# Scores of one head over all 128 rows, plain products for twelve units, globals' outputs in DRAM, and a new order

## The chip, the cores and the metric

The kernel runs on one core of a Trainium2 chip. TensorE multiplies matrices, VectorE and ScalarE do elementwise work, GpSimd helps with some of it, and SyncE (SP) issues most of the DMAs. The metric is the device time of one execution in microseconds (us); the time quoted is the median of several.

## What is computed

Attention for 8 batches of 8 heads, with 512 local and 32 global positions of 64 elements each, followed by a two-layer network over all 4352 tokens. Local queries see the local keys within 32 positions and all global keys; global queries see every key.

```python
k_all = np.concatenate([k_g, k_l], axis=2)
v_all = np.concatenate([v_g, v_l], axis=2)
s_g = scale * np.matmul(q_g, k_all.transpose(0, 1, 3, 2))
out_g = np.matmul(sm(s_g), v_all)
s_ll = scale * np.matmul(q_l, k_l.transpose(0, 1, 3, 2))
s_ll = np.where(np.abs(pos[:, None] - pos[None, :]) <= 32, s_ll, -1e9)
s_l = np.concatenate([scale * np.matmul(q_l, k_g.transpose(0, 1, 3, 2)), s_ll], axis=-1)
out_l = np.matmul(sm(s_l), v_all)
attn_out = np.concatenate([out_g, out_l], axis=2)        # sm is the softmax
x = attn_out.transpose(0, 2, 1, 3).reshape(B * S, H * D) # 4352 x 512
out = gelu(x @ w_in) @ w_out                             # 512 -> 2048 -> 512
```

## The kernel before

**Units and pieces.** A unit is a batch, a half of its 512 local positions and a pair of heads: 64 units, four to a block of 256 tokens. A piece of the network is one such block, 16 of them, and a last one ("g") of the 256 global tokens. In the network, `ml_hc` makes hidden tiles of 256 columns and `ml_o` the outputs of 512 columns; each product is done three times, since an operand is split into a high part in a fast format (`F32R`) and a low part that holds the rest: high by high, high by low, low by high.

**Attention of a unit.** `st_tk` and `st_tq` transpose keys and queries (for the first eight units, `st_tkn` and `st_tqn` do it on TensorE). `st_k1` and `st_q1` copy the high parts, `st_k2` and `st_q2` subtract to get the low parts; the four lie in one tile `kq`, held once. A head's 64 elements fill half of the 128 rows, so the two heads of a pair lie one above the other. `st_s` makes the scores: two windows of 192 and 224 keys, three products, two heads, so twelve products over 64 rows each, alternating between the upper and lower rows. `st_m` masks and takes the extreme, `st_e` exponentiates, `st_n`, `st_nf`, `st_ns` normalise, `st_t` transposes the weights in seven steps, `st_ah` and `st_al` split them, `st_vc` and `st_vl` split the values, `st_o` multiplies in two groups of four products, and `st_c` and `st_x` add the parts. `st_sg` makes the scores of the global queries over the same keys with two products, from `gs`, which holds high and low parts of the queries of both heads with zeros between.

**Plain units.** Units 0 to `NF32` - 1 (the first 8) keep 32-bit operands instead: one plain product in place of three, by `st_q0`, `st_k0`, `st_s` with its `prods` of one pair, `st_sg0`, `st_a0`, `st_o0` and `st_c0`. There is no split on VectorE or ScalarE and no adding up.

**Globals.** `gu_min` to `gu_yl` finish the global queries of a batch, two heads at a time. `gu_yl` adds its last two parts straight into `xg`, a tile that lives until piece "g" reads it (`ml_xh`).

**Weights.** They come as 64-bit numbers (512 KB per DMA, 32 of them by `w_load`), are rebuilt by `w_1` and `w_2` on ScalarE and `w_3` on VectorE, and split by `w_4` and `w_5`. All are used from the first piece on, so they are all prepared in the first tenth of the run.

**The order.** Nothing is ordered by hand. `step` gives each step its engines, durations (`DUR`), due time (with offsets in `OFF`, `OFF0`, `UO`, `WO`, `XO`), needs, the buffers that it takes and frees, and for DMAs a number of issues and a `size`. A planner then simulates all engines and the DMA, picks the ready step due first on each, and fixes one order per engine. An engine executes that order strictly: a step that waits holds up what is behind it. `AHEAD`, `FA`, `PW` and `PU` place attention against the network.

Of the kernel before, what the change touches and what calls it, by code (L numbers as in the profile page):

```python
# [19 lines left out]
NB = 10  # L20
# [39 lines left out]
}  # L60
OFF0 = {
# [7 lines left out]
PW = 7.45  # L69
PA = 14.0  # L70
UO = [-392.3, -324.5, -466.6, -352.7, -219.4, -4.3, 79.2, -212.3, 297.9, -231.0, -224.0, -213.8, -190.2, -142.1, -206.7, -54.7]
WO = [-233.6, -272.1, 18.8, 79.4, -468.3, -440.1, 10.1, -401.7, 160.7, 127.2, 284.8, 552.5, 98.0, 88.9, -36.8, -133.1, -19.5, 157.0, 203.3, 10.3, 3.9, -137.0, -448.4, 17.1, -86.0, 50.4, 66.1, -73.3, 84.2, -14.7, -33.4, 3.9]
FA = 122.95
PU = 9.25
NF32 = 8
# [22 lines left out]
    ('gagl', (0, 0)): -47.6, ('gagl', (0, 1)): 17.8, ('gah', (0, 0), 0): 36.0, ('gah', (0, 0), 1): 34.5,  # L98
    ('gah', (0, 1), 0): -22.0, ('gah', (0, 1), 1): 38.1, ('gal', (0, 0), 0): -245.5, ('gal', (0, 0), 1): 91.2,
    ('gal', (0, 1), 0): 137.9, ('gal', (0, 1), 1): 13.8, ('gex', (0, 0)): 53.2, ('gex', (0, 1)): -193.4,  # L100
# [7 lines left out]
    ('glv', (0, 1), 0): 62.5, ('glv', (0, 1), 1): -201.2, ('glv', (1, 0), 0): -62.3, ('glv', (1, 0), 1): -12.2,  # L108
    ('gmin', (0, 0)): 276.7, ('gmin', (0, 1)): -18.9, ('gn', (0, 0)): -31.4, ('gn', (0, 1)): 12.5,
    ('go', (0, 0), 0): 1.7, ('go', (0, 0), 1): 229.8, ('go', (0, 1), 0): -314.7, ('go', (0, 1), 1): -76.3,  # L110
    ('gsh', (0, 0), 0): -60.2, ('gsh', (0, 0), 1): -125.5, ('gsh', (0, 1), 0): -74.6, ('gsh', (0, 1), 1): 15.3,
    ('gsl', (0, 0), 0): 39.4, ('gsl', (0, 0), 1): 83.0, ('gsl', (0, 1), 0): 28.1, ('gsl', (0, 1), 1): -71.6,
    ('gt', (0, 0)): 79.7, ('gt', (0, 1)): -124.9, ('gvc', (0, 0), 0): -116.3, ('gvc', (0, 0), 1): -243.4,
    ('gvc', (0, 1), 0): -55.5, ('gvc', (0, 1), 1): 56.6, ('gvc', (1, 0), 0): 66.2, ('gvl', (0, 0), 0): -40.7,
    ('gvl', (0, 0), 1): -73.6, ('gvl', (0, 1), 0): -2.3, ('gvl', (0, 1), 1): -173.1, ('gvl', (1, 0), 0): 139.3,
    ('gx', (0, 0), 0): -103.3, ('gx', (0, 0), 1): 81.1, ('gx', (0, 1), 0): -105.6, ('gx', (0, 1), 1): 50.1,
    ('gyh', (0, 0), 0): -41.4, ('gyh', (0, 0), 1): 27.2, ('gyh', (0, 1), 0): 248.2, ('gyh', (0, 1), 1): -30.0,
    ('gyl', (0, 0), 0): -233.3, ('gyl', (0, 0), 1): 138.1, ('gyl', (0, 1), 0): 36.2, ('gyl', (0, 1), 1): 43.6,
# [1283 lines left out]
```

## Time and profile before

| | us |
|---|---|
| median of 3 runs | 1043.84 |
| lowest and highest | 1042.81, 1045.48 |
| the profiled execution, its own time | 1045.36 |
| its span, first to last instruction | 1043.6 |

The profiled execution has a mean granted clock of 0.985. Times inside it are counted from the span's start. In a row of a group the first number after the bar is the busy time of all its instructions in us, then the mean of one in ns; then follows the idle time of the engine ahead of them and what ended it. In a time line the columns are start, length (from the first start to the last end, of as many as stand behind "x"), engine, line and operation. Matmuls overlap, so what one costs is read from one start to the next and not from its length.

### The profile page before, as it was taken

To read this page: it belongs to the slowest core of one execution; us is meant where nothing else is said; L and a number is where in the kernel's file an instruction comes from. 1 tells how busy PE (TensorE), PEld (TensorE's weight loads), DVE (VectorE), ACT (ScalarE), POOL (GpSimd) and SP (SyncE) were. 2 spreads that over 40 slices of the span, in tenths; PEclk is the share of its full clock that TensorE was granted. 3 is DMA by queue.
4 is the path that set the end of the run, shared out by engine and by line. 5 is a ranking of instruction groups with operands and counts; after the bars stand their busy time and mean duration, and the time that the engine had idled before them with its cause. 6 is when DMAs were issued, how large, how long until landed. Compare 5 with 4: busy or idle time off the path is not lost.

```text
span 1043.6 us, 21145 instructions
## 1 busy us (share of the span) xinstructions
PE 1014.7 (97%) x7100; PEld 903.6 (87%) x7100; DVE 668.0 (64%) x2046; ACT 749.2 (72%) x1613; POOL 349.6 (33%) x397
## 2 busy tenths in 40 slices
PE   7679999999999999999999999999999999999998
PEld 3468899998899999899899989999899989999897
DVE  5777868874787658775787658785787658641100
ACT  5788878877888678776788678776788678853221
POOL 3022433234233433234232433334232433233121
PEclk9689999999999999999999999999999999999999
DMA  7777232223222222222222232222322232101000
GB/s 192 207 219 253 37 84 49 61 46 82 45 43 60 56 68 44 57 45 60 65 45 61 54 69 42 60 42 60 67 44 58 56 69 50 32 12 32 1 21 21
DMA packets 264796, 69.64 MB, mean 67 GB/s; under 512 B 250096, under 2 KB 258288, under 8 KB 264688
## 3 DMA queue, kind: packets, MB, share of 16 engines
q1 hardware_dynamic: 263536, 67.91, 28.4%
q8 instruction: 56, 0.92, 0.4%
q10 hardware_dynamic: 1152, 0.39, 0.1%
q14 instruction: 52, 0.43, 0.1%
HBM read 59.31 MB, written 8.91 MB: 65 GB/s over the span
## 4 chain that ended last, share of the span: by engine, by line
PE 90%; SPq 3%; DMA 3%; DVE 2%; ACT 1%; issue 1%; DVEq 0%; ACTq 0%
PE h L922 12%; PE acc L954 12%; PE acc L956 12%; PE h L924 12%; PE acc L955 12%; PE h L923 12%; PE o L722 5%; PE s L615 5%; PE t L686 3%; DMA wpair<-in_moe_w_out_dram 2%; PE go L855 2%; PE sg L766 1%; PE t L687 1%; DMA raws<-in_q_l_dram 1%; SPq L459 1%
## 5 line engine op out<-in xcount | busy, mean ns | idle before, releaser
L310 POOL TENSOR_TENSOR gl<-gf,gh 128x512 fp32r<-128x512 f32 x135 | 178.0, 1318 | 410.3 <-ACT gh L300 267.7
L922 PE MATMUL h<-xx,w 128*128 128x256 f32 x1088 | 313.1, 288 | 0.0
L924 PE MATMUL h<-xx,w 128*128 128x256 f32 x1088 | 304.3, 280 | 0.9 <-DVE w L310 0.9
L923 PE MATMUL h<-xx,w 128*128 128x256 f32 x1088 | 303.9, 279 | 0.0
L954 PE MATMUL acc<-w,gh 128*128 128x512 f32 x544 | 219.2, 403 | 0.0
L956 PE MATMUL acc<-w,gh 128*128 128x512 f32 x544 | 214.6, 394 | 0.0
L955 PE MATMUL acc<-w,gl 128*128 128x512 f32 x544 | 214.5, 394 | 0.0
L922 PEld LDWEIGHTS h<-xx,w 128*128 128x128 f32 x1088 | 204.9, 188 | 9.5 <-issue 0.4
L923 PEld LDWEIGHTS h<-xx,w 128*128 128x128 f32 x1088 | 204.9, 188 | 6.6
L924 PEld LDWEIGHTS h<-xx,w 128*128 128x128 f32 x1088 | 204.7, 188 | 1.3 <-DVE w L310 1.3
L479 ACT ACT_TABLE_LOAD x127 | 162.9, 1283 | 2.3
L300 ACT ACTIVATE gh<-gf 128x512 fp32r<-128x512 f32 x108 | 68.2, 632 | 97.2 <-PE acc L956 96.8
L310 POOL TENSOR_TENSOR vs<-vr,vs 128x512 fp32r<-128x512 f32 x56 | 74.5, 1329 | 154.9 <-DVE vs L302 47.5
L956 PEld LDWEIGHTS acc<-w,gh 128*128 128x128 f32 x544 | 102.0, 188 | 24.8
L479 ACT ACTIVATE gf<-h 128x512 f32<-128x512 f32 x136 | 81.2, 597 | 50.6 <-PE h L924 28.4
L954 PEld LDWEIGHTS acc<-w,gh 128*128 128x128 f32 x544 | 102.1, 188 | 14.3 <-issue 0.3
L955 PEld LDWEIGHTS acc<-w,gl 128*128 128x128 f32 x544 | 102.4, 188 | 12.6
L479 ACT ACTIVATE a_t<-a_t,sm 128x192 f32<-128x192 f32 x240 | 110.1, 460 | 2.8 <-DVE sm L634 1.2
L634 DVE CUSTOM_DVE_ANT_0 a_t<-s,mask 128x192 f32<-128x192 f32 x240 | 77.1, 368 | 42.7 <-PE s L615 42.6
L706 DVE TENSOR_TENSOR at<-t,at 128x512 fp32r<-128x512 f32 (+1 forms) x112 | 66.5, 613 | 44.7 <-ACT at L300 44.3
L300 ACT ACTIVATE at<-t 128x512 fp32r<-128x512 f32 (+1 forms) x112 | 58.9, 539 | 22.8 <-PE t L689 16.2
L722 PE MATMUL o<-at,vs 128*128 128x256 f32 x448 | 73.3, 286 | 0.0
(139 smaller groups left out, 1555.4 us busy)
## 6 DMA issues: line engine op xcount, KB each, us to landing
wpair<-in_moe_w_in_dram SPq DMA_DIRECT2D x16, 512.0 KB, 6.2
wpair<-in_moe_w_out_dram SPq DMA_DIRECT2D x16, 512.0 KB, 6.4
raws<-in_v_l_dram SPq DMA_DIRECT2D x64, 128.0 KB, 2.4
out_dram<-ob SPq DMA_DIRECT2D x32, 256.0 KB, 2.3
raws<-in_k_l_dram SPq DMA_DIRECT2D x224, 36.0 KB, 2.0
vr<-in_v_l_dram SPq DMA_DIRECT2D x112, 64.0 KB, 2.2
raws<-in_q_l_dram SPq DMA_DIRECT2D x224, 32.0 KB, 1.9
vr<-in_v_l_dram SPq DMA_DIRECT2D x56, 32.0 KB, 2.2
```

Of the source, the lines that this page charges most:

```text
L300: nc.scalar.activation(out=out, in_=in_, func=AF.Copy)
L310: (nc.vector if e == "v" else nc.gpsimd).tensor_sub(**kw)
L479: nc.scalar.activation(func=func, **kw)
L634: nc.vector.tensor_tensor_reduce(out=a_t[:, j, aoff[half][i]:aoff[half][i] + w], in0=s[:, c:c + w], in1=masks[half][:, c:c + w], scale=-SC ...
L706: nc.vector.tensor_sub(out=at[:, 1], in0=st.pop((u, "t", j))[:, :n * P].rearrange("p (n q) -> p n q", q=P), in1=at.bitcast(F32)[:, 0])
L722: nc.tensor.matmul(out=o[:, :, qsl], lhsT=l.rearrange("p s e -> p (s e)"), rhs=r, start=(n == 0), stop=(n == 3), skip_group_check=True)
L922: nc.tensor.matmul(out=h, lhsT=hi, rhs=xh, start=(c == 0), stop=False, skip_group_check=True)
L923: nc.tensor.matmul(out=h, lhsT=hi, rhs=xl, start=False, stop=False, skip_group_check=True)
L924: nc.tensor.matmul(out=h, lhsT=lo, rhs=xh, start=False, stop=(c == NCC - 1), skip_group_check=True)
L954: nc.tensor.matmul(out=acc[t], lhsT=gh[:, f % 2, tsl], rhs=hi, start=(f == a), stop=False)
L955: nc.tensor.matmul(out=acc[t], lhsT=gl[:, f % 2, tsl], rhs=hi, start=False, stop=False)
L956: nc.tensor.matmul(out=acc[t], lhsT=gh[:, f % 2, tsl], rhs=lo, start=False, stop=(f == b - 1))
```

## The change

Six things are changed.

1. **Scores.** `kq` grows from 2 x 320 + 2 x 256 to 2 x 320 + 4 x 256 columns. For head j, the rows of that head hold the high part of the keys and the other 64 rows the low part. Queries: `q1` has the high part in both halves of the rows (the second copy by the new `st_q3`), `q2` has the low part in the head's own rows and zeros in the others (written once). `q1` times keys then gives high by high and high by low in one product over 128 rows, `q2` times keys the third. So `st_s` does eight products over 128 rows. Each of `st_k1`, `st_k2`, `st_q1`, `st_q2` and `st_q3` becomes two instructions on 64 partitions.
2. **Globals' queries.** `gs` has seven slots of 32 columns with zeros between; the queries of all heads lie on all 128 rows, so `load_g` moves twice the bytes and `st_tg` transposes 256 in place of 128 columns. `st_sg` still does two products.
3. **Plain units.** `NF32` is 12: units 8 to 11 (first half of batch 1) are plain too. They take keys and queries straight from the transposed tiles and values straight from `vr`; `st_tc1` prepares the plain global queries of batch 1.
4. **Globals' outputs.** `gu_yl` adds in place, `gu_w` writes each result of 128 x 32 to DRAM, and one read (`gu_r`) brings all of them into the memory of `vr` before piece "g". `xg` goes.
5. **Planner's prices.** New durations for the changed steps, and larger sizes for the loads of keys, queries and values.
6. **Order.** All offsets are new, as are `AHEAD` (21.61 to 23.43), `FA` (122.95 to 108.93), `PW` (7.45 to 8.01) and `PU` (9.25 to 8.86).

```diff
-    "tk": 0.65, ..., "tg": 0.32, "k1": {"a": 0.47, "v": 0.31}, "k2": 0.5, "q1": {"v": 0.3, "a": 0.41}, "q2": 0.42,
-    "tgh": 0.62, "tgl": 0.77, "s": 0.97, ...
+    "tk": 0.65, ..., "tg": 0.5, "k1": {"a": 0.9, "v": 0.62}, "k2": 1.0, "q1": {"v": 0.6, "a": 0.82}, "q3": {"v": 0.6, "a": 0.82}, "q2": 0.84, ...
+    "tgh": 0.62, "tgl": 0.77, "s": 0.87, ...
-NF32 = 8
+NF32 = 12
...
-            kq = late["kq"] = xp.tile([P, 2 * NB * 32 + 2 * CH], F32R, name="kq", tag="kq")
+            kq = late["kq"] = xp.tile([P, 2 * NB * 32 + 4 * CH], F32R, name="kq", tag="kq")
+            late["k"] = kq[:, 0:2 * NB * 32].rearrange("p (j w) -> p j w", j=2)
...
-    gs = cp.tile([P, NP, P], F32R, name="gs")
+    gs = cp.tile([P, NP, 7, 32], F32R, name="gs")
...
-        late["xg"] = lp.tile([P, NP, CH], F32, name="xg")
...
     def st_q1(e, u):
-        copy(e, keys_queries("q1"), st[u, "qt"])
+        q = keys_queries("q1")
+        for j in range(2):
+            own_, other = head(j)
+            copy(e, q[own_, j], st[u, "qt"][own_])
+
+    def st_q3(e, u):
+        q = keys_queries("q1")
+        for j in range(2):
+            own_, other = head(j)
+            copy(e, q[other, j], st[u, "qt"][own_])
...
     def st_k2(e, u):
-        sub(e, out=late["k2"], in0=st.pop((u, "kt")).rearrange("p c e -> p (c e)"), in1=late["k1"].bitcast(F32))
+        k, t = late["k"], st[u, "xkt"].rearrange("p c e -> p (c e)")
+        for j in range(2):
+            own_, other = head(j)
+            sub(e, out=k[other, j], in0=t[own_], in1=k[own_, j].bitcast(F32))
...
+    def st_tc1(e, b):
+        late["gs1"] = g = xp.tile([P, NP, 2, SG], F32, name="gs1", tag="kq")
+        nc.vector.memset(g, 0.0)
+        for j in range(2):
+            pr = slice(64 * j, 64 * j + 64)
+            copy(e, g[pr, :, j], st["qgt", b][pr, j::2])
...
-            for n, (qq, kk) in enumerate(prods):
+            for n in range(1 if plain else 2):
                 for jj in range(2):
-                    pr = slice(64 * jj, 64 * jj + 64)
-                    nc.tensor.matmul(out=st[u, "s", jj][:, c:c + w], lhsT=qq[pr, qt * P:qt * P + P], rhs=kk[pr, k0:k0 + w],
...
+                    if plain:
+                        pr = slice(64 * jj, 64 * jj + 64)
+                        l, r = st[u, "qt"][pr, qt * P:qt * P + P], st[u, "kt"][pr, k0:k0 + w]
+                    else:
+                        l, r = late["q2" if n else "q1"][:, jj, qt * P:qt * P + P], late["k"][:, jj, k0:k0 + w]
+                    nc.tensor.matmul(out=st[u, "s", jj][:, c:c + w], lhsT=l, rhs=r,
...
-            nc.vector.tensor_add(out=late["xg"][pr, p, b * SG:b * SG + SG], in0=st[g, i, "x"][pr, j, 0, :], in1=st[g, i, "c"][pr])
+            nc.vector.tensor_add(out=st[g, i, "c"][pr], in0=st[g, i, "x"][pr, j, 0, :], in1=st[g, i, "c"][pr])
+
+    def gu_w(e, g, i):
...
+        nc.sync.dma_start(out=late["xgd"][:, p, b * SG:b * SG + SG], in_=st[g, i, "c"])
+
+    def gu_r(e):
+        late["xg"] = vr.rearrange("p s i j e -> p (s i j e)").rearrange("p (n w) -> p n w", n=NP)
+        nc.sync.dma_start(out=late["xg"], in_=late["xgd"])
...
-                step(("lk", u), load_kn, (u, m), LKE[n], s0 - 15.0, [], [], issues=2 + half + 1 + m // 2, size=0.2 * m, ...)
+                step(("lk", u), load_kn, (u, m), LKE[n], s0 - 15.0, [], [], issues=2 + half + 1 + m // 2, size=0.25 * m, ...)
-            step(("lv", u), load_v, (u, NP), LVE[half], f0 - 18.0, [], [], issues=9, size=1.4, ...)
+            step(("lv", u), load_v, (u, NP), LVE[half], f0 - 18.0, [], [], issues=9, size=1.8, ...)
...
+            step(("q3", u), st_q3, (u,), "va", s0 - 2.2, [("tq", u), ("q1", u)], [("q3", u)], qb, port=n >= NPE)
+                step(("gw", g, i), gu_w, (g, i), "s", g0 + 8.0 + 2 * i, [("gyl", g, i)], [], [("gc", (g, i))], issues=1, size=0.02)
```

More of the change, by code (lines that the diff above doesn't have):

```diff
@@ L110 @@
[L110 to L114, printed above, removed]
@@ L365, in keys_queries @@
         if "kq" not in late:
-            kq = late["kq"] = xp.tile([P, 2 * NB * 32 + 2 * CH], F32R, name="kq", tag="kq")
-            late["k1"], late["k2"] = kq[:, 0:NB * 32], kq[:, NB * 32:2 * NB * 32]
-            late["q1"], late["q2"] = (kq[:, 2 * NB * 32 + i * CH:2 * NB * 32 + (i + 1) * CH] for i in range(2))
+            kq = late["kq"] = xp.tile([P, 2 * NB * 32 + 4 * CH], F32R, name="kq", tag="kq")
+            late["k"] = kq[:, 0:2 * NB * 32].rearrange("p (j w) -> p j w", j=2)
+            late["q1"], late["q2"] = (kq[:, 2 * NB * 32 + 2 * i * CH:2 * NB * 32 + 2 * (i + 1) * CH].rearrange("p (j w) -> p j w", j=2) for i in range(2))
+            for j in range(2):
+                pr = slice(64 - 64 * j, 128 - 64 * j)
+                nc.vector.tensor_copy(out=late["q2"][pr, j].rearrange("p (x w) -> p x w", w=32), in_=a_ts[0][pr, 0, 224:256].unsqueeze(1).to_broadcast([64, CH // 32, 32]))
         return late[name]
@@ L484, in st_tk @@
         t = ap_.tile([P, NB, 32], F32, name="kt", tag="kt")
-        st[u, "kt"] = t
+        st[u, "kt" if place.get(u, NF32) < NF32 else "xkt"] = t
+        if (u, "kt") in st:
+            st[u, "kt"] = t.rearrange("p c e -> p (c e)")
         g = 4 + half
@@ L592, in st_tgl @@
         for j in range(2):
-            pr, hi, lo = gsv(j)
-            nc.vector.tensor_sub(out=lo, in0=qgt[pr], in1=hi.bitcast(F32))
+            nc.vector.tensor_sub(out=gs[:, :, 4 * j + 2], in0=qgt[:, j::2], in1=gs.bitcast(F32)[:, :, 4 * j])
+    def st_tc1(e, b):
+        late["gs1"] = g = xp.tile([P, NP, 2, SG], F32, name="gs1", tag="kq")
+        nc.vector.memset(g, 0.0)
+        for j in range(2):
+            pr = slice(64 * j, 64 * j + 64)
+            copy(e, g[pr, :, j], st["qgt", b][pr, j::2])
+        late["gs1"] = g.rearrange("p n j w -> p n (j w)")
     def windows(half):
@@ L609, in st_s @@
         c = 0
-        prods = [(st[u, "qt"], st[u, "kt"])] if (u, "kt") in st else [(late[x], late[y]) for x, y in (("q1", "k1"), ("q2", "k1"), ("q1", "k2"))]
+        plain = (u, "kt") in st
         for i, (k0, w, qt) in enumerate(windows(half)):
-            for n, (qq, kk) in enumerate(prods):
+            for n in range(1 if plain else 2):
                 for jj in range(2):
-                    pr = slice(64 * jj, 64 * jj + 64)
-                    nc.tensor.matmul(out=st[u, "s", jj][:, c:c + w], lhsT=qq[pr, qt * P:qt * P + P], rhs=kk[pr, k0:k0 + w],
-                                     start=(i == 0 and n == 0), stop=(i == 1 and n == len(prods) - 1), skip_group_check=True)
+                    if plain:
[4 more added lines that the diff above has]
+                    nc.tensor.matmul(out=st[u, "s", jj][:, c:c + w], lhsT=l, rhs=r,
+                                     start=(i == 0 and n == 0), stop=(i == 1 and (plain or n == 1)), skip_group_check=True)
             c += w
@@ L755, in st_sg @@
         st[u, "sg"] = s
-        for n, kk in enumerate([st[u, "kt"]] if (u, "kt") in st else [late["k1"], late["k2"]]):
+        for n, kk in enumerate([st[u, "kt"]] if (u, "kt") in st else [late["k"][:, j] for j in range(2)]):
             if half == 0:
@@ L763, in st_sg @@
                 r = 64 * (p % 2)
-                nc.tensor.matmul(out=o[r:r + 64], lhsT=gs0[:, p, :], rhs=rhs, start=True, stop=True)
+                nc.tensor.matmul(out=o[r:r + 64], lhsT=(late["gs1"] if b else gs0)[:, p, :], rhs=rhs, start=True, stop=True)
             else:
-                nc.tensor.matmul(out=o, lhsT=gs[:, p, :], rhs=rhs, start=(n == 0), stop=(n == 1))
+                nc.tensor.matmul(out=o, lhsT=gs[:, p, 3 * n:3 * n + 4].rearrange("p x w -> p (x w)"), rhs=rhs, start=(n == 0), stop=(n == 1))
     def gcols(u):
@@ L1055, in pv @@
             return [(x[0], pu, *x[1:]) for x in names] if pu else []
-        if half == 0 and p == 0 and n < NF32:
+        if half == 0 and p == 0 and n < NPE:
             step(("lg", b), load_g0, (b,), "s", s0 - 12.0, takes=[("gvr", "q")], issues=1, size=0.08, after=("lk", u))
@@ L1066, in attn_mlp @@
             step(("tgl", b), st_tgl, (b,), "v", s0 - 5.0, [("tgh", b)], [], [("qt", ("g", b))])
+            if n < NF32:
+                step(("tc1", b), st_tc1, (b,), "v", s0 - 5.2, [("tg", b), ("tq", units[3])], [], [("qt", ("g", b))], dur="tgl")
         pair = units[n - 1] if odd else u
@@ L1072, in attn_mlp @@
                 z = units[n - 1 - units[n - 1][2] % (2 if units[n - 1][1] in QUAD else 4)] if n else None
-                step(("lk", u), load_kn, (u, m), LKE[n], s0 - 15.0, [], [], issues=2 + half + 1 + m // 2, size=0.2 * m, after=("lk", z) if n else None)
-                step(("lq", u), load_qn, (u, m), LQE[n], s0 - 14.0, [], [], issues=2, size=0.18 * m, after=("lq", z) if n else None)
+                step(("lk", u), load_kn, (u, m), LKE[n], s0 - 15.0, [], [], issues=2 + half + 1 + m // 2, size=0.25 * m, after=("lk", z) if n else None)
+                step(("lq", u), load_qn, (u, m), LQE[n], s0 - 14.0, [], [], issues=2, size=0.22 * m, after=("lq", z) if n else None)
             step(("tk", u), st_tkn, (u,), "t", s0 - 5.0, [("lk", ld)] + pv(("tq",)), [("h", (u, "k"))], dur="tkn")
@@ L1079, in attn_mlp @@
             z = units[n - 1]
-            step(("lk", u), load_k, (u,), "s", s0 - 15.0, [], [("kraw", u)], issues=4, size=0.25, after=("lk", z if n > NPE else units[4]))
-            step(("lq", u), load_q, (u,), "s", s0 - 14.0, [], [("qraw", u)], issues=4, size=0.23, after=("lq", z if n > NPE else units[4]))
+            step(("lk", u), load_k, (u,), "s", s0 - 15.0, [], [("kraw", u)], issues=4, size=0.45, after=("lk", z if n > NPE else units[4]))
+            step(("lq", u), load_q, (u,), "s", s0 - 14.0, [], [("qraw", u)], issues=4, size=0.42, after=("lq", z if n > NPE else units[4]))
             step(("tk", u), st_tk, (u,), "v", s0 - 5.0, [("lk", u), ("lg", b)] + (pv(("tk",)) if n > NPE else []), [("kt", u)], [("kraw", u), ("kgr", b)])
@@ L1086, in attn_mlp @@
         an = "a%d" % (p if n < NPE else odd)
-        step(("k1", u), st_k0 if w else st_k1, (u,), "av", s0 - 4.0, [("tk", u)] + pv(("k1",)) + ([("tq", units[3])] if n == NF32 else []), [("kt0" if w else "k1", u)], kb if w else [], early=n < 8, port=n >= NPE)
-        step(("q1", u), st_q0 if w else st_q1, (u,), "va", s0 - 2.5, [("tq", u)] + pv(("q1",)) + ([("tq", units[3])] if n == NF32 else []), [("qt0" if w else "q1", u)], qb if w else [], early=n < 8, port=n >= NPE)
+        kd, qd = ("k1", u), ("q1", u)
@@ new lines, in attn_mlp @@
+        if n < NPE or not w:
+            late_kq = [("sg", units[NF32 - 1]), ("tq", units[3])] if n == NF32 else []
+            step(kd, st_k0 if w else st_k1, (u,), "av", s0 - 4.0, [("tk", u)] + (pv(("k1",)) if n != NF32 else late_kq), [("kt0" if w else "k1", u)], kb if w else [], early=n < 8, port=n >= NPE, dur="k0" if w else None)
+            step(qd, st_q0 if w else st_q1, (u,), "va", s0 - 2.5, [("tq", u)] + (pv(("q1",)) if n != NF32 else late_kq), [("qt0" if w else "q1", u)], qb if w else [], early=n < 8, port=n >= NPE, dur="q0" if w else None)
+        else:
+            kd, qd = ("tk", u), ("tq", u)
@@ L1094, in attn_mlp @@
         step(("m", u, 0), st_m, (u, 0), "v", s0 + 1.0, [("s", u)] + ([("mask", 1)] if half else []), [], [("s", (u, 0))])
         step(("m", u, 1), st_m, (u, 1), "v", s0 + 1.1, [("s", u), ("m", u, 0)], [], [("s", (u, 1))])
-        step(("sg", u), st_sg, (u,), "t", s0 + 1.0, [("k1" if w else "k2", u), ("tgl", b), ("s", u)], [("acc" if n < NSG else "s", (u, "g"))], [("kt0", u), ("qt", ("gs0", b))] if w else [("k1", u), ("k2", u), ("gs", b)], dur="sg0" if w else None)
+        step(("sg", u), st_sg, (u,), "t", s0 + 1.0, [kd if w else ("k2", u), ("tc1" if w and b else "tgl", b), ("s", u)], [("acc" if n < NSG else "s", (u, "g"))], ([("kt0", u), ("qt", ("gs0", b))] if n < NPE else [("kt", u)]) if w else [("k1", u), ("k2", u), ("gs", b)], dur="sg0" if w else None)
@@ L1166, in prev @@
             return ("xi" if pieces[n - 1][1] else "xh", pk, p) if n else None
+        if key == "g":
+            step(("gr",), gu_r, (), "s", C0 - 40.0, [("gw", (B - 1, x), i) for x in range(2) for i in range(2)] + [("vl", u) for u in units[-2:]], issues=1, size=0.52)
         for p in range(NP):
@@ L1176, in attn_mlp @@
                 step(("xl", key, p), ml_xl0, (key, p), "v", C0 - 29.9 + 0.1 * p, [("xh", key, p)], [], [("t", (u, "o0"))], dur="xl0")
-            src = [("gyl", (B - 1, x), 1) for x in range(2)] + [("gyl", (B - 1, x), 0) for x in range(2)] if key == "g" else [("x", (*key, p), 1)]
+            src = [("gr",)] if key == "g" else [("x", (*key, p), 1)]
             if n:
```

102 lines of the change are left out of this document (55 added, 47 removed), and 278 rows, old and new, of tables (DUR, OFF, OFF0, XO).

## The prediction

> **What bounds the kernel now.** I read the page first: busy time, then the forty slices.
>
> ```profile
> PE 1014.7 (97%) x7100; PEld 903.6 (87%) x7100; DVE 668.0 (64%) x2046; ACT 749.2 (72%) x1613; POOL 349.6 (33%) x397
> ...
> PE   7679999999999999999999999999999999999998
> ...
> PEclk9689999999999999999999999999999999999999
> DMA  7777232223222222222222232222322232101000
> ```
>
> TensorE is full from the fourth slice on, at full clock; only the first three slices (78 us) have holes, with a low clock (9, 6, 8) and the DMA engines at seven tenths. A busy TensorE need not be at its pace, so the second view sums engines over stretches that I cut at the start of the hole-free part and, in the steady part, at one batch (two blocks: the product of scores at 411.59 us comes back at 529.40).
>
> ```profile
> 0.00:70.00 70.00, 47.38 (x264) 30.78 (x265) 46.36 (x143) 48.63 (x115) 15.57 (x47) 0.78 0.83 226
> 70.00:130.00 60.00, 57.95 (x424) 51.53 (x424) 47.79 (x88) 52.70 (x85) 21.17 (x13) 1.00 0.45 130
> ...
> 411.59:529.40 117.81, 117.81 (x843) 106.51 (x843) 82.65 (x266) 89.79 (x198) 42.23 (x48) 1.00 0.27 55
> ```
>
> Columns: length, then busy time of TensorE, its weight loads, VectorE, ScalarE and GpSimd, the clock, the DMA share and GB/s. In the batch weight loads are busy 106.51 of 117.81 us, 0.904, with no gap in TensorE. By that yardstick 70 to 130 us holds 51.53 / 0.904 = 57.0 us of work: 3.0 us lost. The first 70 us hold at most 30.78 / 0.904 = 34 us: some 36 us lost. Everything between is TensorE's own work. So three things count: what one unit costs TensorE in the steady part, how long the start takes, and whether VectorE (82.65 / 117.81 = 70%) and ScalarE (76%) can still keep ahead.
>
> What a unit costs is read from the distances of starts in the time line of TensorE.
>
> ```profile
> 540.92 0.28 PE L924 MATMUL h<-xx,w 128*128 128x256 f32 x1
> 541.04 0.38 PE L686 MATMUL t<-ident,a_t 128*128 128x128 f32 x2
> 541.26 0.27 PE L687 MATMUL t<-ident,ge 128*128 128x128 f32 x1
> 541.37 0.27 PE L689 MATMUL t<-ident,ge 128*128 128x128 f32 x1
> 541.57 0.93 PE L615 MATMUL s<-kq 64*128 64x192 f32 x12
> 542.43 0.44 PE L686 MATMUL t<-ident,a_t 128*128 128x128 f32 x2
> ...
> 543.99 0.39 PE L956 MATMUL acc<-w,gh 128*128 128x512 f32 x1
> 544.22 0.40 PE L766 MATMUL sg<-kq,gs 128*128 128x256 f32 x2
> 544.46 0.28 PE L922 MATMUL h<-xx,w 128*128 128x256 f32 x1
> ...
> 549.16 0.64 PE L722 MATMUL o<-at,vs 128*128 128x256 f32 x4
> 549.64 0.40 PE L954 MATMUL acc<-w,gh 128*128 128x512 f32 x1
> ```
>
> A product of 512 columns takes 0.23, one of 256 takes 0.12, and a transpose of 128 columns still 0.11: below 256 columns something else than columns sets the pace. The scores' twelve products over 64 rows take 0.86 from first start to the next work, and the transpose ahead of them (541.37 to 541.57) took 0.20 in place of 0.11, so the block costs 0.95. The globals' scores cost 0.24, each of the two output groups 0.48.
>
> **The change part by part.** *Scores over 128 rows.* Twelve products of 64 rows become eight of 128, with 192 and 224 columns, for 52 units (12 to 63). No row shows such a product. The transposes' 0.11 is the nearest: 8 x 0.11 = 0.88, and the change of row grouping, with its 0.09, goes. That saves 0.07 a unit, 52 x 0.07 = 3.6 us. Ends: at the 256-column pace (0.117) 0.94, saving 0.5 us in all; at the columns' own pace (0.23 less 0.12 over 256 columns, 0.45 ns each: 0.09 and 0.10) 0.77, saving 9.5 us. I take 3.6, the row it is nearest to. The globals' scores keep two full products.
>
> One rule speaks against this part. The Trainium skill, "TensorEngine Tiling (Array Packing)", Overview, says that products contracting over at most 64 rows can run as two tiles at once, "up to 2×"; by that alone twelve cost six slots, 0.66, and eight full ones are 0.2 dearer, 11 us over 52 units. The same page, Key Properties, says that changing the tiling mode drains the array. This trace has the measured total, 0.95, in which the switching is contained, so I give the first rule alone no chance.
>
> *Plain products for units 8 to 11.* What these cost shows in the first eight units.
>
> ```profile
> 19.31 0.70 PE L764 MATMUL sg<-kq,gs 128*64 128x288 f32 x2
> 19.94 0.44 PE L532 MATMUL qp<-ident,vr 128*128 128x128 f32 x2
> ...
> 55.50 0.97 PE L615 MATMUL s<-kq 64*128 64x192 f32 x8
> 56.40 0.44 PE L686 MATMUL t<-ident,a_t 128*128 128x128 f32 x2
> ...
> 85.19 1.09 PE L735 MATMUL o<-ao,vre 128*64 128x128 f32 x16
> 86.22 0.50 PE L954 MATMUL acc<-w,gh 128*128 128x512 f32 x1
> ```
>
> Scores 0.90, globals 0.63, outputs 1.03, each with 0.09 for the change of grouping: 2.83. The split unit costs 0.95 + 0.27 (288 columns) + 2 x 0.48 = 2.18. Four units: + 2.6 us on TensorE. These units run beyond about 100 us, where it is nearly full, so I count all of it. In exchange VectorE and ScalarE lose k1, k2, q1, q2 (by the rows below 0.33 + 0.63 + 0.30 + 0.44 = 1.7 us), the two low parts of the attention weights (at most 2 x 0.68), and the four adds of the outputs (4 x 0.42): some 4.7 us a unit, 19 us over both engines between about 85 and 150 us. There only 3.0 us are lost, so at most that is returned; I take 0.5.
>
> *More work for VectorE and ScalarE per split unit.*
>
> ```profile
> L310 DVE TENSOR_TENSOR kq<-kt,kq 128x320 fp32r<-128x320 f32 x56 | 35.3, 630 | 3.4
> L310 DVE TENSOR_TENSOR kq<-qt,kq 128x256 fp32r<-128x256 f32 x56 | 24.4, 436 | 1.1
> L302 DVE CAST kq<-kt 128x320 fp32r<-128x320 f32 x48 | 16.0, 334 | 11.9 <-PE sg L766 11.8
> L302 DVE CAST kq<-qt 128x256 fp32r<-128x256 f32 x32 | 9.5, 297 | 32.4 <-PE s L615 32.2
> L747 DVE TENSOR_TENSOR xs<-o,xs 64x256 f32<-64x256 f32 x112 | 46.6, 416 | 36.0 <-ACT xs L742 34.1
> L706 DVE TENSOR_TENSOR at<-t,at 128x512 fp32r<-128x512 f32 x56 | 38.2, 683 | 33.0 <-ACT at L300 32.7
> ```
>
> A step on 64 partitions takes what one on 128 takes (416 against 436 ns at 256 columns), so halving the partitions doubles the cost: k1 + 0.33, k2 + 0.63, q1 + 0.30, q2 + 0.44, and q3 new with 0.60: 2.3 us a unit, 18.4 a batch. Some of it will go to ScalarE at a little more. Both engines together go from 172.4 to 191 of 2 x 117 us: 82%. The work is done ahead of TensorE, and what hides it is the 117 us of a batch. If that cover tears, k2 (now 1.26) and q2 stand in VectorE's queue ahead of the masked scores, whose bank TensorE then lacks. I take + 0.5 us in all; ends 0 and + 12 (the rival below).
>
> *Globals' outputs through DRAM.* The add into the long tile becomes an add in place of the same size, plus 32 writes of 16 KB and one read of 512 KB on SP.
>
> ```profile
> 954.75 0.39 DVE L883 TENSOR_TENSOR xg<-gx,gc 64x32 f32<-64x32 f32 x2 [1.78 <-ACT gc L877]
> ...
> 985.32 0.40 ACT L300 ACTIVATE xx<-xg 128x256 fp32r<-128x256 f32 x1
> ```
>
> ```profile
> SPq L839 <- POOL vgs L310: 74.5, 14, 25.5
> ```
>
> ```profile
> wpair<-in_moe_w_out_dram SPq DMA_DIRECT2D x16, 512.0 KB, 6.4
> ```
>
> From the last add to its first use there are 30 us; a write of about 2 and a read of 6.4 fit in that. Each write waits for VectorE at the head of SP's queue, with the loads of later units behind it; SP already stands up to 25.5 us for the globals' values without a hole in TensorE. Cost nothing; without that slack, one late load per batch, a few us. The doubled queries of the globals (four DMAs of twice the size and one transpose of 256 in place of 128 columns, once a batch), the one-off zeros and the copies for batch 1 are below 0.3 us a batch on engines with room: nothing.
>
> *New order and larger DMA sizes in the planner.* The start loses its time in waits like this one:
>
> ```profile
> 60.83 1.10 ACT L341 ACTIVATE wpair<-wpair 128x1024 int32<-128x1024 uint16 x1 [3.70 <-DMA wpair<-in_moe_w_out_dram]
> ...
> 64.16 1.98 PE L735 MATMUL o<-ao,vre 128*64 128x128 f32 x16 [4.82 <-ACT ao L300]
> ```
>
> ScalarE stood 3.70 us for a weight's DMA with the exponentials and the copy for TensorE queued behind it; TensorE waited 4.82 and its clock fell, so the same sixteen products took 1.98 in place of 1.09. The diff raises the sizes by which the planner places loads (k 0.20 to 0.25, v 1.4 to 1.8), so it expects weights later and would put such a step behind the exponentials. Of the 36 us lost this one wait and its cold stretch carry some 7. I take a gain of 3.0, under half of it; ends 10 gained and 4 lost, since every step of the start is placed anew and a similar wait can arise elsewhere.
>
> **Sum.** - 3.6 + 2.6 - 0.5 + 0.5 - 3.0 = - 4.0 us on the profiled execution: a span of 1043.6, its own time 1045.36, with 1.8 around the span. That run is 1.5 above the median of 1043.84 (0.15%); applied to the median: 1039.8.
>
> **Rivals.**
> 1. *Cover torn (slower).* In a busy half batch both helpers are fuller:
>
> ```profile
> 397.00:457.00 60.00, 60.00 (x436) 54.05 (x435) 46.79 (x146) 48.76 (x105) 19.67 (x23) 1.00 0.25 50
> ```
>
>    Four units there add 9.2 us: if all of it fell on VectorE, 56.0 of 60. If TensorE then waits once a block for the added half of a k2 (0.63), with 13 blocks: + 8.2, 1048.0; from about 0.55 a block on the result is over the 0.3% (3.1 us) that a measurement of this kernel can tell from no change. Against it: 9 points of spare on both engines together, and no block waits now.
> 2. *Nothing at the start.* The steady gain and the plain units' price nearly cancel (- 3.6 + 2.6) and the new order brings no more than 0.3: 1042.5, within 0.3%. For it: the first loads are DMA-bound at 0.83 whatever the order.
> 3. *The start yields more.* Both this wait and others go, 10 in place of 3.0: 1032.8.
> 4. *Columns set the pace of the 128-row products:* 9.5 in place of 3.6: 1033.9. Against it: no product here runs below 0.11. The Trainium skill, "TensorE: Matmul & The Clock Gate", Back-to-back issue gap, gives N / 2.4 + 2.5 ns for isolated products, 0.08 to 0.10 us at these widths, which would bring the same; the 0.11 of the transposes disagrees.
>
> **How the numbers follow.** Forecast 0.37, torn cover 0.17, nothing at the start 0.23, more at the start 0.15, columns 0.08. The range takes in all but the worse part of the torn cover and the best of the start: 1031 to 1047.5. Faster by over 0.3% (below 1040.7): 0.30 of the forecast's 0.37 and rivals 3 and 4, 0.53; slower 0.18; within, 0.29.
>
> **What would show it.** The scores' block: 0.88 and the next start 0.11 after a transpose, not 0.20. A batch: 117.3 us in place of 117.81, with no gaps at TensorE; gaps released by VectorE or ScalarE mean rival 1. The first 70 us: fewer gaps ahead of the outputs' products at 64 us. The forecast is wrong if the 128-row products take 0.117 or more, if SP's waits for the globals delay loads, or if the new start is worse than the old.

## The result, and the profile after

| | before | after |
|---|---|---|
| median, us | 1043.78 (4 runs, 1042.81 to 1045.48) | 1035.78 (4 runs, 1034.41 to 1036.76) |
| the profiled execution's own time | 1045.36 | 1035.02 |
| its span | 1043.6 | 1033.2 |
| its mean granted clock | 0.985 | 0.990 |

The ratio is 0.9921 (95% interval 0.9902 to 0.9939): 8 us faster, where 4 were forecast. The spans differ by more, 10.4 us, since the profiled run of before was 1.6 above its median and that of after 0.8 below its own.

The page after, with the busy lines of TensorE and then the same slices as before (busy tenths, granted clock, DMA share):

```profile
PE 1011.6 (98%) x6908; PEld 909.9 (88%) x6908; DVE 734.2 (71%) x2169; ACT 814.9 (79%) x1761; POOL 352.8 (34%) x399
...
PE   7789999999999999999999999999999999999998
...
PEclk9789999999999999999999999999999999999999
DMA  8869213333223232323222332323222332111000
```

TensorE has 192 products fewer and is still the bound. VectorE and ScalarE together have 132 us more to do, and neither has made a hole in the later slices. The stretches of the kernel after, in the columns of the prediction's windows:

```profile
0.00:70.00 70.00, 54.65 (x325) 36.11 (x325) 49.25 (x146) 50.66 (x119) 24.80 (x54) 0.88 0.77 202
70.00:130.00 60.00, 58.16 (x401) 50.91 (x402) 45.45 (x80) 51.96 (x83) 21.58 (x18) 0.97 0.57 173
...
411.59:529.40 117.81, 117.81 (x812) 108.35 (x811) 89.36 (x283) 101.85 (x223) 41.34 (x46) 1.00 0.27 57
```

The steady part is as gapless as before, at 76% of VectorE and 86% of ScalarE. Its yardstick is now 108.35 / 117.81 = 0.920 of weight-load time. By that the first 70 us hold 36.11 / 0.920 = 39.3 us of work: 30.7 lost, where 36 were. From 70 to 130 us 50.91 / 0.920 = 55.3: 4.7 lost, where 3.0 were. By this estimate the start gained some 5 and gave some 2 back.

The rest is in the steady part. Two blocks of scores of TensorE's time line that stand four batches apart, after:

```profile
350.26 1.15 PE L646 MATMUL s<-kq 128*128 128x192 f32 x8
...
816.75 1.15 PE L646 MATMUL s<-kq 128*128 128x192 f32 x8
```

and two that stand three batches apart in the kernel before:

```profile
411.59 0.93 PE L615 MATMUL s<-kq 64*128 64x192 f32 x12
...
765.03 0.93 PE L615 MATMUL s<-kq 64*128 64x192 f32 x12
```

A batch took 353.44 / 3 = 117.81 us and takes 466.49 / 4 = 116.62. That is 1.19 for eight units, 0.149 a unit, and twice the 0.07 that was forecast.

### The profile page after: what moved, and what is told of

Its sections match the earlier page's. It is cut to its first block, busy times and chain, and to the rows that moved or that the text cites. A ratio compares the mean times of both kernels' runs of the same rounds, so it can differ in the third digit from the quotient of the medians.

```text
span 1033.2 us, 21240 instructions
## 1 busy us (share of the span) xinstructions
PE 1011.6 (98%) x6908; PEld 909.9 (88%) x6908; DVE 734.2 (71%) x2169; ACT 814.9 (79%) x1761; POOL 352.8 (34%) x399
## 4 chain that ended last, share of the span: by engine, by line
PE 93%; SPq 2%; DMA 2%; DVE 1%; ACT 1%; issue 0%; POOL 0%; ACTq 0%; DVEq 0%
PE h L963 12%; PE h L965 12%; PE h L964 12%; PE acc L995 12%; PE acc L996 12%; PE acc L997 12%; PE s L646 5%; PE o L753 5%; PE t L717 3%; PE go L886 2%; DMA wpair<-in_moe_w_out_dram 2%; PE sg L797 1%; PE t L718 1%; PE o L766 1%; PE gt L847 1%; PE t L720 1%
## 5 line engine op out<-in xcount | busy, mean ns | idle before, releaser
L995 PEld LDWEIGHTS acc<-w,gh 128*128 128x128 f32 x544 | 102.2, 188 | 12.9 <-issue 0.3
L311 POOL TENSOR_TENSOR vs<-vr,vs 128x512 fp32r<-128x512 f32 x52 | 68.5, 1317 | 105.1 <-DVE vs L303 47.1
L737 DVE TENSOR_TENSOR at<-t,at 128x512 fp32r<-128x512 f32 (+1 forms) x104 | 62.5, 615 | 28.3 <-ACT at L301 27.9
L301 ACT ACTIVATE at<-t 128x512 fp32r<-128x512 f32 (+1 forms) x104 | 54.1, 540 | 32.2 <-PE t L718 15.7
L311 POOL TENSOR_TENSOR vgs<-raws,vgs 128x640 fp32r<-128x640 f32 x32 | 51.1, 1597 | 77.3 <-ACT vgs L301 68.5
```

Source lines behind the costliest of these rows:

```text
L301: nc.scalar.activation(out=out, in_=in_, func=AF.Copy)
L311: (nc.vector if e == "v" else nc.gpsimd).tensor_sub(**kw)
L737: nc.vector.tensor_sub(out=at[:, 1], in0=st.pop((u, "t", j))[:, :n * P].rearrange("p (n q) -> p n q", q=P), in1=at.bitcast(F32)[:, 0])
L995: nc.tensor.matmul(out=acc[t], lhsT=gh[:, f % 2, tsl], rhs=hi, start=(f == a), stop=False)
```

## The experiments

Two theories stood at the outset. **The first:** a block of 64-row products has a price that the prediction did not see, so the scores alone bring 7 to 8 us, and all the rest of the change comes to nothing. **The rival:** the scores bring the 3.6 of the prediction, and the start brings the other 7, against the 2.6 that the plain units cost. A third question was whether the price is one of the products or of the change between row groupings, and further runs took single terms of the sum.

### The scores over 64 rows again, in the order of after

```diff
-            for n in range(1 if plain else 2):
+            parts = [("q1", 0)] if plain else [("q1", 0), ("q2", 0), ("q2", 0)]
+            for n, (qq, side) in enumerate(parts):
...
-                        l, r = late["q2" if n else "q1"][:, jj, qt * P:qt * P + P], late["k"][:, jj, k0:k0 + w]
+                        pr = head(jj)[side] if side < 2 else slice(0, P)
+                        l, r = late[qq][pr, jj, qt * P:qt * P + P], late["k"][pr, jj, k0:k0 + w]
```

> The changed kernel in its own order, but the scores of the 52 split units again as twelve products over 64 rows (the third product repeats the second, since the low keys lie on the other rows; the low-keys term is left out). Theory A, the row grouping costs more than the prediction counted: in the profile of before the product that follows the block takes 0.11 us longer too, so twelve cost 1.04 us and eight over 128 rows 0.895. Then this kernel is 52 x 0.145 = 7.5 us slower than the changed one (about 1043.3 us). Theory B, the prediction's 0.07 a unit: 3.6 us slower (about 1039.4), and the rest of the gain lies in the order.

Measured: 1044.25 us (10 runs), 0.9996 of before (0.9986 to 1.0005). The profiled span is 1040.9, 7.7 over that of after. As after stands at 0.9921, the eight products are worth (0.9996 - 0.9921) x 1044 = 7.8 us, some 2 us either way by the two intervals, and everything else in the change together is 0.4 us, which is nothing that can be told from zero. From 240 to 930 us this run has 4934 products, exactly as many as before, so in the steady part nothing but the scores moves the time. The rival falls.

### How the price splits: four products of 64 rows, and four of 128

The same loop, with one part in place of two: the first run takes `[("q1", 0)]`, four products over 64 rows, and the second `[("q1", 2)]`, four over 128.

> The changed kernel with only the high-by-high scores of the split units, as four products over 64 rows (both low parts are left out of the scores). With e1 it gives the price of a pair of products and of the change of row grouping: theory A: 1.04 - 4 x 0.11 = 0.60 us a block, of which 0.38 do not depend on the number of products. Theory B: 0.95 - 0.44 = 0.51, with 0.29 of it fixed.

> The changed kernel with only the first of the two 128-row products of each window (the low queries are left out): four products in place of eight. Theory A: 4 x 0.112 = 0.45 us a block with no fixed part, so the span falls by 52 x 0.45 = 23 us unless VectorE or ScalarE become the bound. A rival: a fixed part is in the 0.895 too, then the block takes more than half of it, and the span falls less.

Measured: 1022.63 and 1018.47 us, one execution each. The blocks are read from the time line of TensorE, from the network's product ahead of a block to the second one behind it, less those two at 0.117 each. Before, twelve products over 64 rows:

```profile
411.38 0.28 PE L924 MATMUL h<-xx,w 128*128 128x256 f32 x1
411.59 0.93 PE L615 MATMUL s<-kq 64*128 64x192 f32 x12
412.44 0.38 PE L922 MATMUL h<-xx,w 128*128 128x256 f32 x1
412.67 0.28 PE L923 MATMUL h<-xx,w 128*128 128x256 f32 x1
```

Four over 64 rows:

```profile
515.71 0.28 PE L967 MATMUL h<-xx,w 128*128 128x256 f32 x1
515.92 0.48 PE L648 MATMUL s<-kq 64*128 64x192 f32 x4
516.33 0.38 PE L965 MATMUL h<-xx,w 128*128 128x256 f32 x1
516.55 0.28 PE L966 MATMUL h<-xx,w 128*128 128x256 f32 x1
```

After, eight over 128 rows:

```profile
521.88 0.28 PE L965 MATMUL h<-xx,w 128*128 128x256 f32 x1
521.99 1.04 PE L646 MATMUL s<-kq 128*128 128x192 f32 x8
522.88 0.29 PE L963 MATMUL h<-xx,w 128*128 128x256 f32 x1
523.00 0.28 PE L964 MATMUL h<-xx,w 128*128 128x256 f32 x1
```

Four over 128 rows:

```profile
513.46 0.28 PE L967 MATMUL h<-xx,w 128*128 128x256 f32 x1
513.58 0.60 PE L648 MATMUL s<-kq 128*128 128x192 f32 x4
514.02 0.29 PE L965 MATMUL h<-xx,w 128*128 128x256 f32 x1
514.14 0.28 PE L966 MATMUL h<-xx,w 128*128 128x256 f32 x1
```

| block | from, to | less 2 x 0.117 |
|---|---|---|
| 12 over 64 rows | 411.38, 412.67 | 1.06 |
| 4 over 64 rows | 515.71, 516.55 | 0.61 |
| 8 over 128 rows | 521.88, 523.00 | 0.89 |
| 4 over 128 rows | 513.46, 514.14 | 0.45 |

Eight more products over 64 rows cost 0.45: 0.113 for each pair, so the pair, upper and lower rows, does run together. Six pairs would be 0.68; the block takes 1.06, so 0.38 is a fixed price. Four more over 128 rows cost 0.44, 0.11 each, with no fixed price. The place to see it is the product *behind* the block: from 412.44 to 412.67 it holds TensorE for 0.23, twice its usual 0.117, and after a block of 128 rows only for 0.12. The entry, 411.38 to 411.59, is the other 0.09 that shows.

The weight loads show what is different there. Before:

```profile
411.26 0.19 PEld L924 LDWEIGHTS h<-xx,w 128*128 128x128 f32 x1
411.59 0.74 PEld L615 LDWEIGHTS s<-kq 64*128 64x128 f32 x12
412.44 0.19 PEld L922 LDWEIGHTS h<-xx,w 128*128 128x128 f32 x1
```

After:

```profile
521.88 0.97 PEld L646 LDWEIGHTS s<-kq 128*128 128x128 f32 x8
```

The loads at 411.26 and 521.88 start 0.11 to 0.12 ahead of their products (411.38 and 521.99). At the two edges of the 64-row block the load starts together with its product (411.59 and 412.44), so nothing covers it. Two single loads of 0.19 come to 0.38; that they are the whole price is argued, not tested.

The Trainium skill, "TensorEngine Tiling (Array Packing)", Overview, promises up to twice the speed where at most 64 rows are contracted, and Key Properties says that a change of the tiling mode drains TensorE. The 0.113 a pair agrees with the first; the 0.38 a block is in line with the second, though no run tells a drain from the uncovered loads. Six slots with the change are dearer than eight without.

The second run gained less against after than its blocks: 52 x 0.44 = 23 us were to be had, and 1033.2 - 1016.7 = 16.5 came. Part of the difference is lost in the first 70 us (weight loads 33.64 us where after has 36.11), and from 240 to 930 us TensorE has 2.3 us of gaps, 1.4 of them behind VectorE, where after has none. That the work of VectorE begins to bind at this pace is likely, but not shown by one execution.

### The plain units, 8 in place of 12

`NF32 = 8` in the kernel after, first with its offsets as they are, then with offsets that were searched anew for 8.

> The changed kernel with units 8 to 11 split again (8 plain units), planned anew with the same offsets. By the prediction's price TensorE has 2.6 us less to do (more by the price that counts what follows a change of grouping), and VectorE and ScalarE 19 us or more to do between 85 and 150 us. If that stretch has room: 2 to 3 us faster than the changed kernel, about 1033. If the plain units are what keeps it full: TensorE's lost time between 70 and 150 us grows by more than 3 us, and it is the same or slower, 1036 to 1042.

> Eight plain units again in the changed kernel, as in e4, but with the offsets of the order searched anew for that case, since e4 with the offsets made for twelve lost its time in a bad order. If the plain units 8 to 11 are worth their 3.5 us on TensorE by relieving VectorE and ScalarE: slower than the changed kernel by 4 us or more, 1040 to 1046, with TensorE's lost time ahead of 150 us grown. If not: 1032 to 1036. Kept in mind: the search for this case was shorter than whatever made the offsets of the two given kernels, so a slower result only shows that no better order was found.

Measured: 1081.81 us, 1.0356 of before (1.0341 to 1.0372), and 1048.2 us, 1.0044 (1.0031 to 1.0058); the kernel after was run again beside the second:

> The changed kernel as it is, on the same chip as the kernel with 128-column stationary operands for the globals' plain scores: 1034 to 1037.

It took 1036.8 us, 0.9925 (0.9912 to 0.9939). The first says little about plain units, since its offsets were made for 12: it loses 12.5 and 12.9 us in the stretches of 30 us from 70 and from 100 us on (weight loads of 16.12 and 15.77 us, over 0.920). The second is 12 us slower than after, but its search was shorter than the one that after came from, so 12 is an upper bound of what four plain units bring to the kernel after, not their value.

### The relief that four plain units give

The kernel after, with 17.7 us of VectorE work added in units 8 to 11: steps that they have are repeated, with the same result.

```diff
+        for o, i in kin * (2 if u in units[NPE:NF32] else 1):
...
+        for _ in range(3 if u in units[NPE:NF32] else 1):
+            nc.vector.transpose(out=t, in_=qraw.rearrange("p c e -> p (c e)"))
...
+        if u not in first8:
+            copy("v", at, t)
...
+        if u not in first8:
+            for _ in range(4):
+                copy("v", xs[:, u[2]], o)
```

> The changed kernel in its own order, with 17.7 us of work put back on VectorE for the four plain units 8 to 11 (4.4 us each: copies and transposes done again onto the same place), about what plain products took from VectorE and ScalarE there. If that relief is what lets the start and the stretch to 150 us run full: 3 us or more slower than the changed kernel (1039 or more). If the stretch has room: within 1 us of it (1035 to 1037), and the plain units only cost TensorE their 3.5 us.

Measured: 1048.1 us, 1.0028 of before (1.0011 to 1.0046): some 11 us over after. The windows of this run,

```profile
100.00:130.00 30.00, 27.83 (x166) 23.76 (x164) 24.00 (x44) 20.84 (x39) 10.47 (x9) 0.94 0.22 61
...
170.00:240.00 70.00, 65.42 (x443) 58.89 (x443) 62.26 (x181) 50.84 (x118) 23.91 (x29) 0.98 0.29 58
```

and of after:

```profile
100.00:130.00 30.00, 29.70 (x199) 26.27 (x199) 21.10 (x43) 22.42 (x44) 12.28 (x11) 1.00 0.24 59
...
170.00:240.00 70.00, 69.85 (x488) 63.83 (x488) 60.29 (x174) 55.55 (x126) 27.58 (x30) 1.00 0.30 60
```

Weight loads fall by 2.5 and 4.9 us there, so 8 us of TensorE's work is lost. VectorE is at 89% of the last stretch, where after has 86%. The losses stand close behind the added steps. The last of them are the copies of `st_c0` (five here, four of them added), and TensorE's longest wait of this stretch follows:

```profile
181.72 2.25 DVE L303 COPY xs<-o 128x256 f32<-128x256 f32 x5
...
184.12 0.41 PE L719 MATMUL t<-ident,a_t 128*128 128x128 f32 x2 [1.91 <-DVE xs L303]
```

From 190 to 240 us TensorE has no gap again. So in this order, and at these places in VectorE's queue, work of the size that the plain units save costs most of itself. The same work at other places was not tried.

### The wait for a weight at 60 us, alone

The kernel before, its order kept but for one step: the first step of weight pair 10 (`w_1`) goes behind the exponentials and the copy that stood behind it on ScalarE.

```diff
+    names = [e[2]["name"] for e in order]
+    order.insert(names.index(("w2", 10)) - 1, order.pop(names.index(("w1", 10))))
```

> The kernel of before, with one step moved in ScalarE's order: the first rebuilding step of the sixth weight, for whose DMA ScalarE stood 3.70 us at 57 us of the profile, goes behind the exponentials and the copy that were queued behind it, directly ahead of that weight's second step. Theory A, waits like this one are what a new order can take from the start: TensorE's wait of 4.82 us ahead of the outputs' products and the cold clock behind it shrink, 3 to 5 us faster than before (1039 to 1041). Theory B, the start is bound by the loads whatever stands behind them: the wait moves to the next weight, within 1 us of before.

Measured: 0.9973 of before (0.9957 to 0.9990), 2.8 us, with an interval from 1.0 to 4.5: more than the second theory allows, and just short of the 3 to 5 of the first. The wait of 4.82 is gone from TensorE's time line, and the sixteen products after it take 1.09 in place of 1.98:

```profile
60.32 1.09 PE L735 MATMUL o<-ao,vre 128*64 128x128 f32 x16 [0.64 <-ACT ao L300]
```

The window from 40 to 70 us, in this run

```profile
40.00:70.00 30.00, 24.34 (x185) 18.71 (x184) 24.54 (x72) 24.57 (x52) 6.53 (x9) 0.85 0.83 240
```

and before:

```profile
40.00:70.00 30.00, 21.56 (x147) 16.06 (x148) 21.32 (x69) 22.12 (x50) 6.51 (x9) 0.73 0.82 243
```

Weight loads rise by 2.65, which is 2.9 us of work, and the clock from 0.73 to 0.85; from 70 to 130 us they fall by 2.2, since other steps come late. The slow stretch has also moved rather than gone: a wait of 1.41 for VectorE follows at 62.83, and up to 66.3 us products of 256 columns stand 0.21 apart in place of 0.117. So the wait was worth some 2.8, not the 7 that it seemed to carry.

### The added work of VectorE and ScalarE, in the order of before

The kernel before with ten steps on 64 partitions where it had four on 128; the scores as before.

```diff
+    halves = (slice(0, 64), slice(64, 128))
...
-        copy(e, keys_queries("q1"), st[u, "qt"])
+        for _ in range(2):
+            for pr in halves:
+                copy(e, keys_queries("q1")[pr], st[u, "qt"][pr])
...
+        for pr in halves:
+            sub(e, out=late["q2"][pr], in0=q[pr], in1=late["q1"][pr].bitcast(F32))
```

and likewise `k1` and `k2`.

> The kernel before, in its own order, with the change's added work outside TensorE alone: k1, k2, q1 and q2 are each written by two instructions over 64 rows, and q1 a second time into the other rows; the scores keep their twelve products over 64 rows. The forecast took this work as covered, at +0.5 us with ends of 0 and +12. Theory A, the cover holds (VectorE busy 77% and ScalarE 81% of the span have room for it, and a block of products does not wait): within 1.5 us of the kernel before, 1042 to 1046, and no new gap of TensorE from 240 us on. Theory B, the cover is torn in an order that was not made for it: 1049 or more, with TensorE waiting for the low parts or for what stands behind them.

Measured: 1108.08 us, 1.0616 of before (1.0599 to 1.0634): 64 us slower, far beyond the end of 12 as well. The windows of this run,

```profile
240.00:930.00 690.00, 667.10 (x4623) 591.27 (x4623) 539.98 (x1640) 516.97 (x1142) 237.89 (x260) 0.99 0.25 52
```

and of after:

```profile
240.00:930.00 690.00, 690.00 (x4798) 636.51 (x4797) 553.75 (x1682) 605.50 (x1324) 245.44 (x269) 1.00 0.27 55
```

Both helpers are *less* busy than in the kernel after, and yet TensorE waits. VectorE's time line shows for what; this run behind one block of scores:

```profile
551.27 1.25 DVE L302 CAST kq<-qt 64x256 fp32r<-64x256 f32 x4 [0.29 <-PE s L624]
552.55 0.87 DVE L310 TENSOR_TENSOR kq<-qt,kq 64x256 fp32r<-64x256 f32 x2
553.46 0.36 DVE L643 CUSTOM_DVE_ANT_0 a_t<-s,mask 128x192 f32<-128x192 f32 x1
```

and before:

```profile
542.54 0.29 DVE L302 CAST kq<-qt 128x256 fp32r<-128x256 f32 x1 [1.91 <-PE s L615]
542.87 0.42 DVE L310 TENSOR_TENSOR kq<-qt,kq 128x256 fp32r<-128x256 f32 x1
543.21 0.35 DVE L634 CUSTOM_DVE_ANT_0 a_t<-s,mask 128x192 f32<-128x192 f32 x1
```

In this order the next unit's queries are split between a block's last product and its masked scores. That took 0.67 us and takes 2.19, the masked scores free their bank 1.5 us later, and TensorE stands for it. The waits of TensorE from 240 to 930 us, longest sum first:

```profile
PE sg L775 <- DVE sm L643: 7.2, 13, 0.9
PE gtg L826 <- DVE xs L757: 6.6, 5, 1.3
PE o L731 <- DVE at L715: 4.7, 6, 1.5
```

All gaps there come to 22.9 us. The masked scores are the largest part, but only a third; the next two are waits for other steps of VectorE. 4623 products ran where before had 4934, 6% fewer, which is 43 us. The rest of that is not visible as gaps, and some 15 us more were lost ahead of 240 us (1377 products where before had 1484).

With the same twelve products and the same ten steps a unit, but in the order made for them (and with 12 plain units), the first experiment took 1044.25. The plain units run ahead of 180 us, so they do not explain the stretch from 240 us on. So the work is not hidden by its share of the engine; it is hidden by the order, which also fixes the engine of each step: of the copies of the queries' high part 128 of 224 run on VectorE here, and 42 of 208 in the kernel after.

### Globals' scores of the plain units over all 128 columns

A cheaper form of one block, in the kernel after: the stationary operand takes the queries of two pairs, so that the output is whole and the column grouping stays.

```diff
-                r = 64 * (p % 2)
-                nc.tensor.matmul(out=o[r:r + 64], lhsT=(late["gs1"] if b else gs0)[:, p, :], rhs=rhs, start=True, stop=True)
+                g2 = (late["gs1"] if b else gs0)[:, p - p % 2:p - p % 2 + 2, :]
+                nc.tensor.matmul(out=o, lhsT=g2.rearrange("p n w -> p (n w)"), rhs=rhs, start=True, stop=True)
```

> The changed kernel with the globals' plain scores (12 units) using the 128 columns of a pair of units as the stationary operand in place of 64, so that TensorE keeps one tiling for them; the 64 rows of the result that belong to the other unit aren't read. If a change of tiling costs some 0.25 us per block as it does for the scores over 64 rows, four such blocks in the full stretch give 1 us, and up to 3 with those of the start: 1033 to 1035. If the loading of 128 columns of 32-bit numbers costs as much: no difference.

> The kernel of e7 beside the changed one on the same chip. If keeping one tiling saves 0.25 us in each of the four blocks in the full stretch: 1 us faster than the changed kernel, 0.1%. If what is saved in the start is lost again in waits: no difference.

Measured: 1035.16 us, 0.9899 (0.9879 to 0.9919), and 1035.06, 0.9921 (0.9907 to 0.9934), beside 0.9921 and 0.9925 of after. TensorE is busy 4.0 us less (1007.6), and 2.5 us less in the two runs side by side. In the time line the block falls from 0.83 to 0.49, by 0.34. Eight of the 12 blocks lie in the start, where TensorE is not the bound; the other four would give 1.4 us, less than the intervals can show. It cannot be told from after.

## Why the prediction came out as it did

| term | forecast | measured | from |
|---|---|---|---|
| scores over 128 rows | - 3.6 | - 7.8 | first experiment |
| plain units 8 to 11 | + 2.6 | + 3.5 | blocks in the time line |
| all the rest: relief, added work, start | - 3.0 | - 3.9 | what is left of the total |
| sum | - 4.0 | - 8.2 | 0.9921 x 1043.78 |

**Scores: the mechanism right, the size half.** The step "the block costs 0.95" is the one that failed. It took the distance from the block to the next start and the longer entry, and stopped there. The product behind the block was not looked at, though the row 542.43 was in the prediction's own fence: the two transposes that start there last 0.44, two others in the same fence 0.38. The 0.06 between them belongs to the block, and 0.11 where a network product stands behind it (412.44 to 412.67). So the block costs 1.06, or some 1.0 next to transposes. Eight products over 128 rows were forecast at 0.88 and take 0.89. With 0.149 a unit for 0.07, 52 units give 7.8.

**Plain units: the same oversight, on the other side.** The sums 2.83 and 2.18 leave out the product behind each block too. In after the outputs' block reads

```profile
94.90 0.40 PE L997 MATMUL acc<-w,gh 128*128 128x512 f32 x1
95.23 1.09 PE L766 MATMUL o<-ao,vr 128*64 128x128 f32 x16
96.25 0.38 PE L963 MATMUL h<-xx,w 128*128 128x256 f32 x1
96.47 0.29 PE L964 MATMUL h<-xx,w 128*128 128x256 f32 x1
```

which is 1.57 less 0.233 and 0.117: 1.22. Scores and globals read 1.10 and 0.83 in the same way, 3.15 a plain unit; a split unit of before 1.06 + 0.27 + 0.95 = 2.28. Four units: + 3.5, or 0.2 less, since in one of them scores and outputs stand side by side (145.60 and 146.51) and share a change. The two oversights had opposite signs, but there are 52 units of the one and 4 of the other.

**The relief: 0.5 was argued wrongly.** "Only 3.0 us are lost, so at most that is returned" holds for the order of before with its own work in it. It does not bound what the stretch would lose with more, and added work there cost 11 us. The run with 8 plain units (at most 12) sets only a bound. What the relief is worth on its own was not isolated. So that the last row of the table comes out near its forecast, - 3.9 for - 3.0, is in part luck: its terms were not measured one by one.

**The added work: 0.5 for the cover, and none was needed,** for another reason than the one given. TensorE's waits from 240 to 930 us are none in the kernel after (690.00 of 690.00), as forecast. But "9 points of spare" is not what holds the cover: with that spare the same work in the order of before cost 64 us. The mechanism of the first rival, steps in VectorE's queue ahead of the masked scores, is real, and was priced by its busy time where its place decides. In the kernel after 166 of the 208 copies of the queries' high part run on ScalarE:

```profile
L301 ACT ACTIVATE kq<-qt 64x256 fp32r<-64x256 f32 x166 | 68.9, 415 | 10.1 <-PE s L646 7.0
```

The amount of work came out as forecast: 89.36 + 101.85 = 191.2 us in the window of a batch, where 191 was expected. Halving the partitions does not halve the time. VectorE's steps after:

```profile
L311 DVE TENSOR_TENSOR kq<-kt,kq 64x320 fp32r<-64x320 f32 x104 | 53.7, 517 | 3.1
L311 DVE TENSOR_TENSOR kq<-qt,kq 64x256 fp32r<-64x256 f32 x104 | 48.1, 462 | 2.0
```

At 320 columns it is 517 ns where 630 was taken, a fifth less; at 256 columns 462 where 436 was.

**The start: 3.0 taken; it gained some 5 by 70 us and gave 2 back by 130.** The forecast rested on one wait, and that wait, moved alone, is worth 2.8 (1.0 to 4.5). So the second rival (nothing at the start) and the third (10) fall. How much of the gain is the order, how much the larger loads and how much the relief stays open: the old parts in the new order, and the new parts in the old, were not tried, since the two orders have different steps.

**Globals through DRAM: nothing, as forecast.** The last write and the read in the time line, issue times:

```profile
937.27 0.32 SPq L920 DMA_DIRECT2D xgd<-gc  x1
938.81 0.32 SPq L924 DMA_DIRECT2D vr<-xgd  x1
```

A write lands in 1.6 us, the read in 3.6, and the first use starts at 977.1, 35 us after it. SP stood 38.4 us for these writes, the longest 19.2, with no gap of TensorE in the steady part.

**Columns as the pace (the fourth rival) falls.** Its time, 1033.9, was nearer than the forecast, but products with 192 and 224 columns take 0.11, not 0.09 and 0.10. The formula of the Trainium skill, "TensorE: Matmul & The Clock Gate", Back-to-back issue gap, which is for isolated products, does not give the pace of these. The section LDWEIGHTS of the same page of the Trainium skill gives columns / 1.2 ns for a weight load, an estimate of 107 ns for 128; the pace of 0.11 is close to that, but a single load lasts 0.19 in this trace, so that the loads set the pace is not shown. The sum of this rival was also a little off: by its own 0.45 ns a column the eight products come to 0.75, not 0.77, and save 10 us.

## What to carry to other kernels

Read what a block costs from the last undisturbed start ahead of it to the *second* start behind it; what a change of row or column grouping costs may stand in the follower. Six slots of packed products with a change of grouping can be dearer than eight full ones, and by these figures packing pays against the same products one by one only from four pairs in one go (an estimate: 0.38 + 4 x 0.113 = 0.83 for 8 x 0.11 = 0.88). And the share of an engine says whether work fits, not whether it is hidden: where the order on that engine is fixed, ask which step stands behind the added one, and who waits for it.

## What the runs showed of the hardware that was not expected

- A block of 64-row products between 128-row ones costs 0.38 us beside its pairs: 0.09 at the entry, 0.11 in the product behind it, and the rest inside. At both edges the weight load starts with its product and not 0.11 ahead of it. The pairs themselves run together, 0.113 each.
- With twelve products and with four the entry takes 0.21 (411.38 to 411.59, 515.71 to 515.92) and the product behind 0.22 to 0.23, so the cost is one of the change and not of the products.
- The same ten steps a unit on VectorE and ScalarE cost nothing that can be told in one order and 64 us in another, at 78% of VectorE and 75% of ScalarE in the slow one and 80% and 88% in the fast.
